# A mixture-of-experts kernel: slots from the third unit on, three picked last slots, and another order of scatters on GpSimd

## The chip, the core and the metric

The kernel runs on one core of one Trainium2 chip. The metric is the device time of one execution in microseconds (us). A run of three or five rounds alternates the kernel studied with the kernel before on the same chip. A ratio is the mean time of one kernel's runs over that of the other's in the same rounds, so it is not quite the ratio of the medians that are quoted beside it.

## The reference, cut to what matters

```python
# x: (8, 3584, 192) float32; a causal depthwise convolution of width 7, softmaxed weights per head
x = attn(x, weight).reshape(28672, 192)
e_idx  = argmax(x @ w_gate, axis=1)                    # 8 experts, one per row
gate_w = softmax(x @ w_gate)[row, e_idx]
eom    = sigmoid(x @ w_output_gate)
for e in range(8):
    mask = e_idx == e
    out[mask] = gate_w * eom[:, e] * (relu(x[mask] @ w1[e]) @ w2[e])     # 192 -> 1024 -> 192
```

## The kernel before

The rows are worked on in 16 units of 1792 rows. For each unit a *front* computes the convolution and the gates (front_a), then ranks the rows by expert and scatters them as pairs of rows, eight scatters a unit, to a stream in DRAM that is sorted by expert (front_b). A *slot* loads 512 rows of one expert from that stream with a transposing DMA (xa, xb), runs the two layers on TensorE and scatters 4 times 128 rows to the output. A unit's iteration has four slots, each in four quarters, with the fronts of later units between the quarters:

```python
for u in range(1, NU):                      # NU = 16; unit 0 and 1 are prepared before
    todo = []
    for e, bap, inv in plans.pop(u):        # four slots; eight after the last unit
        base = reg(bap, [ET.SP], E * CAP - TT)
        todo.append((e, inv, slot_load(base, u)))
    fa = front_a(u + 2) ...
    fb = front_b(u + 1) ...
    for k, (e, inv, xab) in enumerate(todo):
        s = Slot(xab, w_at(e * WE), inv)
        for q in range(4):
            s.first(q)                      # first layer, a quarter
            drain(fa, 1)
            if prev is not None:
                prev.second(q)              # second layer of the slot before; output scatters
            drain(fb, 1)                    # may make the data of one input scatter
        prev = s
```

All scatters are issued by GpSimd, in program order. Before, a made input scatter was put into a queue and issued one at a time ahead of an output scatter:

```python
                for j in (q - 1, q):        # in second(q), q odd
                    emit_in()               # at most one waiting input scatter
                    i = nc.gpsimd.indirect_dma_start(out=out, ..., in_=self.y[:, j, :])
```

A slot's load waits until all scatters of its unit have landed. Rows left after the static slots go through a loop whose count is known only at run time: it picks the expert with most rows left, computes one slot with nothing beside it, and repeats.

## Time and profile before

| | before |
|---|---|
| median of 3 runs (lowest to highest) | 780.03 us (779.94 to 781.78) |
| profiled run, span | 772.0 us |
| TensorE busy, mean granted clock | 655.4 us (85%), 0.947 |
| first slot matmul | 86.1 us |
| last matmul of the static slots | 742.1 us |
| last output scatter issued | 764.88 us |

The main stage lies between the first slot matmul and the last matmul of the static slots. Ahead of it is the start-up, after it the loop's one pass.

### The profile page before, as it was taken

The page shows a single profiled execution, that of the slowest core. Times are in us where ns is not written, and L with a number is a line of the kernel's source. Part 1 is how long each engine was busy: PE and PEld are TensorE (multiplying, and loading weights), DVE is VectorE, ACT ScalarE, POOL GpSimd, SP SyncE. Part 2 cuts the span into 40 slices and gives each one's busy share as a digit, 9 for nine tenths or more (in the row PEclk, how much of TensorE's full clock was granted, in tenths as well). Part 3 has the DMA queues.
Part 4 walks back from the last instruction along what each step waited for, and adds up shares of the span by engine and source line. Part 5 has one row for each costly group of instructions (what it writes and reads, how often), then busy time and mean ns, then how long its engine had stood idle before and what let it go on. Part 6 is the DMA issues. An engine that isn't in the chain of part 4 may idle for free. (4 is left out here: it accounts for less than half of the span.)

```text
span 772.0 us, 14134 instructions
## 1 busy us (share of the span) xinstructions
PE 655.4 (85%) x4948; PEld 436.2 (57%) x4948; DVE 406.5 (53%) x1298; ACT 366.5 (47%) x581; POOL 411.5 (53%) x425
## 2 busy tenths in 40 slices
PE   3866498989989898989989898989989898869953
PEld 1524165665757475656747475656757575547632
DVE  7425183836566383837556383837566474802220
ACT  0657153554535363545536364545546354436621
POOL 1436145473747465473737465563737375656652
PEclk9978599999999999999999999999999999989987
DMA  7999933253535343252535343442532313234110
GB/s 152 231 238 203 142 101 108 72 160 75 144 102 143 103 133 104 69 155 73 152 92 139 99 127 106 101 133 62 157 88 74 93 61 110 70 102 114 48 41 9
DMA packets 132359, 86.59 MB, mean 112 GB/s; under 512 B 88427, under 2 KB 122455, under 8 KB 132288
## 3 DMA queue, kind: packets, MB, share of 16 engines
q1 hardware_dynamic: 102656, 42.35, 23.4%
q0 software_dynamic: 28736, 43.31, 20.5%
q8 instruction: 39, 0.64, 0.4%
q14 instruction: 32, 0.26, 0.1%
q10 hardware_dynamic: 896, 0.03, 0.1%
HBM read 35.80 MB, written 44.43 MB: 104 GB/s over the span
## 5 line engine op out<-in xcount | busy, mean ns | idle before, releaser
L579 POOL DMA_INDIRECT out_dram<-y,oi x260 | 262.7, 1011 | 242.1 <-issue 179.0
L547 ACT ACTIVATE ht<-pp 128x1024 f16<-128x1024 f32 x195 | 199.3, 1022 | 183.9 <-PE pp L541 183.9
L539 PE MATMUL pp<-xa,wres 128*128 128x512 f16 x520 | 203.0, 390 | 61.1 <-DMA xa<-xcg_sorted 61.1
L558 PE MATMUL pyt<-wres,ht 128*128 128x192 f16 (+1 forms) x2080 | 220.9, 250 | 2.9 <-DVE ht L545 2.9
L558 PEld LDWEIGHTS <-ht 128*128 128x128 f16 x2080 | 182.7, 99 | 67.1 <-issue 37.0
L541 PE MATMUL pp<-xb,wres 128*128 128x512 f16 x520 | 202.2, 389 | 12.2 <-DMA xb<-xcg_sorted 12.2
L457 POOL DMA_INDIRECT xcg_sorted<-xs,du x128 | 130.1, 1017 | 89.4 <-ACT xs L278 42.2
L290 PE MATMUL pf<-xt,band 118*112 118x384 f32 x256 | 115.3, 543 | 19.5 <-DMA xt<-in_x_dram 14.1
L539 PEld LDWEIGHTS <-wres 128*128 128x128 f16 (+1 forms) x520 | 51.4, 99 | 112.4 <-DMA xa<-xcg_sorted 41.2
L545 DVE TENSOR_SCALAR ht<-pp 128x1024 f16<-128x1024 f32 x65 | 79.2, 1219 | 59.2 <-PE pp L541 59.2
L569 ACT COPY y<-pyt 128x384 f32<-128x384 f32 x130 | 62.4, 480 | 93.9 <-PE pyt L558 84.1
L280 DVE COPY cv<-pf 112x384 f32<-112x384 f32 x54 | 29.2, 541 | 89.3 <-PE pf L290 89.3
L290 PEld LDWEIGHTS pf<-xt,band 118*112 118x112 f32 x256 | 48.0, 195 | 48.9 <-DVE band L133 13.6
L541 PEld LDWEIGHTS <-wres 128*128 128x128 f16 (+1 forms) x520 | 51.8, 100 | 37.6 <-issue 8.2
L572 DVE TENSOR_SCALAR oi<-pyt 128x4 uint32<-128x4 f32 x65 | 10.5, 162 | 115.8 <-ACT y L569 110.3
L439 PE MATMUL pf<-xrow,pm 112*128 112x194 f16 x512 | 64.6, 247 | 6.9 <-DVE pm L423 4.5
L418 DVE TENSOR_TENSOR xrow<-cv,gs 112x384 f16<-112x384 f32 x128 | 64.7, 545 | 0.0
L423 DVE TENSOR_SCALAR pm<-pos,pos 112x256 f16<-112x256 f16 x256 | 64.6, 324 | 0.0
L304 PEld LDWEIGHTS pf<-identf,cv 112*128 112x128 f32 x384 | 43.6, 141 | 17.4 <-DVE cv L280 2.2
L278 ACT COPY cv<-pf 112x384 f32<-112x384 f32 x74 | 33.9, 479 | 40.1 <-PE pf L290 25.0
L304 PE MATMUL pf<-identf,cv 112*128 112x112 f32 x384 | 51.5, 260 | 0.5 <-ACT cv L278 0.4
L278 ACT CAST xs<-pf 128x388 f16<-128x388 f32 x76 | 37.2, 489 | 28.8 <-PE pf L439 20.2
(132 smaller groups left out, 425.0 us busy)
## 6 DMA issues: line engine op xcount, KB each, us to landing
xt<-in_x_dram SPq DMA_DIRECT2D x8, 1344.0 KB
xt<-in_x_dram SPq DMA_DIRECT2D x8, 1260.0 KB
out_dram<-y,oi POOLq DMA_INDIRECT x260, 2.7
wres<-in_moe_w_dram POOLq DMA_DIRECT2D x8, 384.0 KB, 10.5
wres<-in_moe_w_dram POOLq DMA_DIRECT2D x8, 256.0 KB, 11.5
xcg_sorted<-zrow SPq DMA_DIRECT2D x8, 256.0 KB
xcg_sorted<-xs,du POOLq DMA_INDIRECT x128, 3.2
xa<-xcg_sorted SPq DMA_TRANSPOSE x65
```

What stands on the lines that cost most here:

```text
L278: nc.scalar.copy(out=o, in_=i)
L290: nc.tensor.matmul(pc[0:BT, 0:NB * GH], band[0:KI, h, :], xt[0:KI, :, h * GH:(h + 1) * GH], start=True, stop=True)
L304: nc.tensor.matmul(pt[:, j * BT:(j + 1) * BT], cvf[0:BT, m * 2 * D + i * 128:m * 2 * D + (i + 1) * 128], identf[0:BT, 0:BT], is_transpose= ...
L418: nc.vector.tensor_tensor(out=xr[P, k:k + 2, 0:D], in0=cv[P, k:k + 2, :], in1=gs[P, k:k + 2].unsqueeze(2).to_broadcast([BT, 2, D]), op=ALU ...
L423: nc.vector.tensor_scalar(out=pms[i][P, l, :], in0=pos16[P], scalar1=pos[P, l * NG + i:l * NG + i + 1], scalar2=None, op0=ALU.is_equal)
L457: i = nc.gpsimd.indirect_dma_start(out=xcg2, out_offset=bass.IndirectOffsetOnAxis(ap=du[:, i:i + 1], axis=0), in_=xs.rearrange("p r w -> p ...
L539: nc.tensor.matmul(pp[:, j, :], self.w(fc * 128, 128), self.xa, start=True, stop=False)
L541: nc.tensor.matmul(pp[:, j, :], self.w(F + fc * 128, 128), self.xb, start=False, stop=True)
L545: nc.vector.tensor_relu(out=ht, in_=pp)
L547: nc.scalar.activation(out=ht, in_=pp, func=AF.Relu)
L558: nc.tensor.matmul(self.pp[:, o:o + D], self.ht[fc // 2][:, fc % 2, q * 128:(q + 1) * 128], self.w(2 * F + fc * D, D), start=(fc == 0 and ...
L579: i = nc.gpsimd.indirect_dma_start(out=out, out_offset=bass.IndirectOffsetOnAxis(ap=self.oi[:, j:j + 1], axis=0), in_=self.y[:, j, :], in_ ...
```

## The change

The slots begin with the third unit (U0 = 2), so that they are fuller; the three last slots are picked among the experts with most rows left, in the overlapped part of the program; GpSimd gets its scatters in the order in which their data is made. There are twelve buffers (xs) for input scatters in place of six, and the experts' weights are issued two at a time in place of four and then two.

```diff
-    NXS = 6
+    NXS = 12
...
+    def emit_out():
+        while pout:
+            y, oi, j = pout.popleft()
+            i = nc.gpsimd.indirect_dma_start(out=out, ..., in_=y[:, j, :], ...)
...
+    U0 = 2
     def plan(u):
-        if u == 0:
+        if u < U0:
             return []
-        p = plan_half((u + 1) % 2, "a")
+        p = plan_half(u % 2, "a")
...
-    for u in range(2):                     # fronts ahead of all slots
+    for u in range(U0 + 1):
...
-        if u == 0:
-            for e in range(EH, EH + 2):
-                load_w(e)
+        if u < U0:
+            load_w(2 + 2 * u)
+            load_w(3 + 2 * u)
...
-    for u in range(1, NU):
+    for u in range(U0, NU):
...
+        if u == NU - 1:
+            for sel, bap, inv in [pick() for _ in range(ND)]:          # ND = 3
+                base = reg(bap[0:1, 0:1], [ET.SP], E * CAP - TT)
+                todo.append((sel, inv, slot_load(base, u)))
...
                 if prev is not None:
                     prev.second(q)
+                    emit_out()
                 drain(fb, 1)
+                emit_in(len(pend))
```

pick() is the arithmetic that stood in the loop's body, on VectorE; the loop stays for what is left.

More of the change, by code (lines that the diff above doesn't have):

```diff
@@ L60 @@
     WE = F + F + FCH * D
+    ND = 3
     BIG = float(1 << 30)
@@ L201, with load_w @@
     nc.vector.tensor_copy(out=pos16, in_=poi.rearrange("p r j -> p (r j)"))
+    wres = const.tile([128, E * WE], FP16)
+    def load_w(e):
+        o = e * WE
+        nc.gpsimd.dma_start(wres[:, o:o + F], moe_w1[e, 0:128, :])
+        nc.gpsimd.dma_start(wres[0:64, o + F:o + 2 * F], moe_w1[e, 128:D, :])
+        nc.gpsimd.dma_start(
+            wres[:, o + 2 * F:o + WE].rearrange("p (c d) -> p c d", d=D),
+            moe_w2[e].rearrange("(c p) d -> p c d", p=128))
+    load_w(0)
     GE = NG * E
@@ L244 @@
     nc.vector.memset(zrow, 0.0)
-    wres = const.tile([128, E * WE], FP16)
-    def load_w(e):
-        o = e * WE
-        nc.gpsimd.dma_start(wres[:, o:o + F], moe_w1[e, 0:128, :])
-        nc.gpsimd.dma_start(wres[0:64, o + F:o + 2 * F], moe_w1[e, 128:D, :])
-        nc.gpsimd.dma_start(
-            wres[:, o + 2 * F:o + WE].rearrange("p (c d) -> p c d", d=D),
-            moe_w2[e].rearrange("(c p) d -> p c d", p=128))
     def zero_w(e):
@@ L469, in emit_in @@
             n -= 1
+    pout = deque()
+    def emit_out():
+        while pout:
+            y, oi, j = pout.popleft()
+            i = nc.gpsimd.indirect_dma_start(
+                out=out, out_offset=bass.IndirectOffsetOnAxis(ap=oi[:, j:j + 1], axis=0),
+                in_=y[:, j, :], in_offset=None, bounds_check=N - 1, oob_is_err=False)
+            nodep(i, "out", ("out",))
+            last[0] = "out"
     def nodep(i, group, others):
@@ L502, in plan_half, with pick @@
         return [(e0 + i, bu[0:1, i:i + 1], iu[:, i, :]) for i in range(EH)]
+    U0 = 2
     def plan(u):
-        if u == 0:
+        if u < U0:
             return []
-        p = plan_half((u + 1) % 2, "a")
+        p = plan_half(u % 2, "a")
         if u == NU - 1:
-            p += plan_half(u % 2, "b")
+            p += plan_half((u + 1) % 2, "b")
         return p
+    def pick():
+        lv = pr.tile([128, E], FP32, tag="lv", name="lv")
+        nc.vector.tensor_tensor(out=lv, in0=R, in1=DN, op=ALU.subtract)
+        lm = pr.tile([128, 1], FP32, tag="lm", name="lm")
+        nc.vector.tensor_reduce(out=lm, in_=lv, axis=AX.X, op=ALU.max)
+        oh = pr.tile([128, E], FP32, tag="oh", name="oh")
+        nc.vector.scalar_tensor_tensor(out=oh, in0=lv, scalar=lm, in1=rev,
+                                       op0=ALU.is_equal, op1=ALU.mult)
+        om = pr.tile([128, 1], FP32, tag="om", name="om")
+        nc.vector.tensor_reduce(out=om, in_=oh, axis=AX.X, op=ALU.max)
+        sel = pr.tile([128, 1], U32, tag="sel", name="sel", bufs=ND)
+        nc.vector.tensor_scalar(out=sel, in0=om, scalar1=-float(WE), scalar2=float(E * WE),
+                                op0=ALU.mult, op1=ALU.add)
+        nc.vector.tensor_scalar(out=oh, in0=oh, scalar1=om, scalar2=None, op0=ALU.is_equal)
+        bt = pr.tile([128, E], FP32, tag="bt", name="bt")
+        nc.vector.scalar_tensor_tensor(out=bt, in0=R, scalar=-float(TP), in1=DN,
+                                       op0=ALU.add, op1=ALU.min)
+        nc.vector.scalar_tensor_tensor(out=bt, in0=bt, scalar=2.0, in1=oh,
+                                       op0=ALU.mult, op1=ALU.mult)
+        bo = pr.tile([128, 1], FP32, tag="bo", name="bo")
+        nc.vector.tensor_reduce(out=bo, in_=bt, axis=AX.X, op=ALU.add)
+        bou = pr.tile([128, 1], U32, tag="bou", name="bou", bufs=ND)
+        nc.vector.tensor_copy(out=bou, in_=bo)
+        tk1 = pr.tile([128, 1], FP32, tag="tk1", name="tk1")
+        nc.vector.tensor_scalar(out=tk1, in0=lm, scalar1=float(TP), scalar2=None, op0=ALU.min)
+        nc.vector.scalar_tensor_tensor(out=DN, in0=oh, scalar=tk1, in1=DN,
+                                       op0=ALU.mult, op1=ALU.add)
+        nc.vector.tensor_scalar(out=tk1, in0=tk1, scalar1=-2.0, scalar2=float(TT),
+                                op0=ALU.mult, op1=ALU.add)
+        iv1 = pr.tile([128, 4], FP32, tag="iv1", name="iv1")
+        nc.vector.tensor_scalar(out=iv1, in0=rowf, scalar1=tk1, scalar2=BIG,
+                                op0=ALU.is_lt, op1=ALU.mult)
+        iu1 = pr.tile([128, 4], U32, tag="iu1", name="iu1", bufs=ND)
+        nc.vector.tensor_copy(out=iu1, in_=iv1)
+        return sel, bou, iu1
@@ L576, in second @@
                                             op=ALU.bitwise_or)
-                for j in (q - 1, q):
-                    emit_in()
-                    i = nc.gpsimd.indirect_dma_start(
-                        out=out, out_offset=bass.IndirectOffsetOnAxis(
-                            ap=self.oi[:, j:j + 1], axis=0),
-                        in_=self.y[:, j, :], in_offset=None,
-                        bounds_check=N - 1, oob_is_err=False)
-                    nodep(i, "out", ("out",))
-                    last[0] = "out"
+                pout.extend((self.y, self.oi, j) for j in (q - 1, q))
     def reg(ap, engines, hi):
@@ L609, in chain @@
             yield from g
-    for e in range(EH):
-        load_w(e)
+    load_w(1)
     drain(front_a(0))
     ze = 0
-    for u in range(2):
+    for u in range(U0 + 1):
         fa, fb = front_a(u + 1), front_b(u)
@@ L626 @@
         emit_in(len(pend))
-        if u == 0:
-            for e in range(EH, EH + 2):
-                load_w(e)
+        if u < U0:
+            load_w(2 + 2 * u)
+            load_w(3 + 2 * u)
     while ze < E:
@@ L639 @@
             base = reg(bap, [ET.SP], E * CAP - TT)
-            todo.append((e, inv, slot_load(base, u)))
+            todo.append((w_at(e * WE), inv, slot_load(base, u)))
+        if u == NU - 1:
+            for sel, bap, inv in [pick() for _ in range(ND)]:
+                base = reg(bap[0:1, 0:1], [ET.SP], E * CAP - TT)
+                todo.append((sel, inv, slot_load(base, u)))
         fa = front_a(u + 2) if u + 2 < NU else iter(())
         fb = front_b(u + 1) if u + 1 < NU else iter(())
-        for k, (e, inv, xab) in enumerate(todo):
-            if u == 1 and k < 2:
-                load_w(EH + 2 + k)
-            s = Slot(xab, w_at(e * WE), inv)
+        for k, (w, inv, xab) in enumerate(todo):
+            if u == U0 and k < 2:
+                load_w(E - 2 + k)
+            if not callable(w):
+                w = w_dyn(reg(w[0:1, 0:1], [ET.PE], (E - 1) * WE))
+            s = Slot(xab, w, inv)
             for q in range(4):
@@ L658 @@
         prev.second(q)
+        emit_out()
     lf = const.tile([128, E], FP32)
@@ L676 @@
     with tc.For_i(0, rn, 1):
-        lv = pr.tile([128, E], FP32, tag="lv", name="lv")
-        nc.vector.tensor_tensor(out=lv, in0=R, in1=DN, op=ALU.subtract)
-        lm = pr.tile([128, 1], FP32, tag="lm", name="lm")
-        nc.vector.tensor_reduce(out=lm, in_=lv, axis=AX.X, op=ALU.max)
-        oh = pr.tile([128, E], FP32, tag="oh", name="oh")
-        nc.vector.scalar_tensor_tensor(out=oh, in0=lv, scalar=lm, in1=rev,
-                                       op0=ALU.is_equal, op1=ALU.mult)
-        om = pr.tile([128, 1], FP32, tag="om", name="om")
-        nc.vector.tensor_reduce(out=om, in_=oh, axis=AX.X, op=ALU.max)
-        sel = pr.tile([128, 1], U32, tag="sel", name="sel")
-        nc.vector.tensor_scalar(out=sel, in0=om, scalar1=-float(WE), scalar2=float(E * WE),
-                                op0=ALU.mult, op1=ALU.add)
-        nc.vector.tensor_scalar(out=oh, in0=oh, scalar1=om, scalar2=None, op0=ALU.is_equal)
-        bt = pr.tile([128, E], FP32, tag="bt", name="bt")
-        nc.vector.scalar_tensor_tensor(out=bt, in0=R, scalar=-float(TP), in1=DN,
-                                       op0=ALU.add, op1=ALU.min)
-        nc.vector.scalar_tensor_tensor(out=bt, in0=bt, scalar=2.0, in1=oh,
-                                       op0=ALU.mult, op1=ALU.mult)
-        bo = pr.tile([128, 1], FP32, tag="bo", name="bo")
-        nc.vector.tensor_reduce(out=bo, in_=bt, axis=AX.X, op=ALU.add)
-        bou = pr.tile([128, 1], U32, tag="bou", name="bou")
-        nc.vector.tensor_copy(out=bou, in_=bo)
-        tk1 = pr.tile([128, 1], FP32, tag="tk1", name="tk1")
-        nc.vector.tensor_scalar(out=tk1, in0=lm, scalar1=float(TP), scalar2=None, op0=ALU.min)
-        nc.vector.scalar_tensor_tensor(out=DN, in0=oh, scalar=tk1, in1=DN,
-                                       op0=ALU.mult, op1=ALU.add)
-        nc.vector.tensor_scalar(out=tk1, in0=tk1, scalar1=-2.0, scalar2=float(TT),
-                                op0=ALU.mult, op1=ALU.add)
-        iv1 = pr.tile([128, 4], FP32, tag="iv1", name="iv1")
-        nc.vector.tensor_scalar(out=iv1, in0=rowf, scalar1=tk1, scalar2=BIG,
-                                op0=ALU.is_lt, op1=ALU.mult)
-        iu1 = pr.tile([128, 4], U32, tag="iu1", name="iu1")
-        nc.vector.tensor_copy(out=iu1, in_=iv1)
+        sel, bou, iu1 = pick()
         base = reg(bou[0:1, 0:1], [ET.SP], E * CAP - TT)
@@ L716 @@
             s.second(q)
+            emit_out()
 _INS = ['x', 'weight', 'moe_w_gate', 'moe_w_output_gate', 'moe_w1', 'moe_w2']
```

## The prediction

> **What bounds the kernel now.** I read the page's header and slices first, then the waits of TensorE, of the other engines and of the DMA queue, then the timeline at three places: the start, one boundary between two units, and the end.
>
> The page:
>
> ```profile
> span 772.0 us, 14134 instructions
> PE 655.4 (85%) x4948; PEld 436.2 (57%) x4948; DVE 406.5 (53%) x1298; ACT 366.5 (47%) x581; POOL 411.5 (53%) x425
> ...
> PE   3866498989989898989989898989989898869953
> ...
> PEclk9978599999999999999999999999999999989987
> DMA  7999933253535343252535343442532313234110
> ```
>
> TensorE sets the pace in the middle, where its slices show 8 and 9. Slices 1 to 5 are a start-up with DMA at 9, and the last two are a tail with everything low. So there are three stages, and each needs its own account.
>
> The waits of the whole run (the last line is from the DMA queue's own list):
>
> ```profile
> POOL out_dram L579 <- issue: 179.0, 164, 13.2
> PE pp L539 <- DMA xa<-xcg_sorted: 61.1, 16, 13.4
> ACT xs L278 <- DMA xcg_sorted<-xs,du: 8.6, 2, 7.4
> ...
> SPq L516 <- DMA xcg_sorted<-xs,du: 253.0, 32, 20.2
> ```
>
> In the main stage TensorE has one big wait: the transposed load of a slot's rows (xa). There are 16 such waits: 13.4 us at the first slot, 7.0 us in the loop at the end, and 14 at the boundaries between units (40.8 us together by the same list cut to 110 to 740 us). The load itself waits for the scatters (xs to xcg_sorted) to land.
>
> One boundary, from the timeline:
>
> ```profile
> 161.92 0.56 DVE L280 CAST xs<-pf 128x388 f16<-128x388 f32 x1 [0.16 <-PE pf L439]
> ...
> 167.96 0.98 POOL L457 DMA_INDIRECT xcg_sorted<-xs,du  x1 [0.30 <-issue]
> ...
> 170.22 0.82 PE L558 MATMUL pyt<-wres,ht 128*128 128x192 f16 x8
> 170.48 1.15 SPq L516 DMA_TRANSPOSE xa<-xcg_sorted  x1
> ...
> 173.67 0.39 PE L539 MATMUL pp<-xa,wres 128*128 128x512 f16 x1 [2.63 <-DMA xa<-xcg_sorted]
> ```
>
> The unit's last scatter data is ready at 162.5. GpSimd issues that scatter only at 167.96: it is 5.5 us behind. The load starts 2.5 us later, and TensorE 3.2 us after that. I read the same five times at the 14 boundaries from 129.9 to 687.2: the lag is 5.3 to 6.1 us, the stall 2.3 to 3.0 us, except 6.4 us at the last one, where the unit has less TensorE work.
>
> The end:
>
> ```profile
> 740.59 1.48 PE L558 MATMUL pyt<-wres,ht 128*128 128x192 f16 x16
> ...
> 746.85 0.98 POOL L579 DMA_INDIRECT out_dram<-y,oi  x1 [0.30 <-issue]
> ...
> 749.07 0.59 PE L539 MATMUL pp<-xa,wres 128*128 128x512 f16 x1 [7.00 <-DMA xa<-xcg_sorted]
> ...
> 759.14 2.14 PE L558 MATMUL pyt<-wres,ht 128*128 x16
> 761.01 1.00 POOL L579 DMA_INDIRECT out_dram<-y,oi  x1 [13.18 <-issue]
> ...
> 764.88 0.98 POOL L579 DMA_INDIRECT out_dram<-y,oi  x1 [0.30 <-issue]
> ```
>
> The static slots end on TensorE at 742.1 and on GpSimd at 746.85. Then the loop runs once, with nothing to overlap it. Its last output scatter is issued at 764.88, and 7.1 us later the span ends.
>
> **What the Trainium skill says.** "Perfetto Trace Analysis", section "DMA Instruction — SWDGE (GPSIMD)": the window shown for such a DMA ends when its descriptors are written, not when data has moved. The trace agrees: 0.98 us shown, 2.4 us at least to landing. "DMA: Bandwidth & Descriptors", section "Two DMAs through the same engine are not ordered": a reader of written data must wait for the writer's completion semaphore. So issue-to-load time (2.5 us here) stays whatever the order. "TensorE: Matmul & The Clock Gate", section "What's actually happening": the array drops to half clock after an idle window of some 3.4 us and needs as long to recover. The trace partly agrees: after this 2.63 us stall eight output matmuls show 1.49 us in place of 0.82, and slot matmuls beyond 0.5 us follow 9 of the 14 boundaries, not all.
>
> **The change part by part.**
>
> *Slots.* I counted the routing of the reference's own inputs: pairs of rows per unit, block group and expert, rounded up, taken off 256 a slot. For the kernel before this gives 64 static slots and one loop pass of 108 pairs: 65, and the page's 260 output scatters are 65 times 4. For the changed kernel: slots begin with unit 2, so 14 units of 4, 4 more after the last, and 3 picked. At the picks 104, 102 and 82 pairs are left with three experts and none with the others. So 63 slots, and the loop runs zero times.
>
> *Main stage.* Before, from the first slot matmul at 86.1 to 742.1 there are 656.0 us: unit 1's iteration 43.8, twelve full ones 517.7 (43.1 each), unit 14's 39.6, unit 15's 54.9 with eight slots. After, unit 1's iteration is gone and three slots are added to the last. A slot costs TensorE 4 times (0.87 + 0.66) = 6.1 us, from start-to-start times in the timeline (161.72 to 162.59 for a quarter's first matmuls, 162.97 to 163.63 for its second). The picked slots address weights by a register. In the loop pass that did so, 16 output matmuls took 2.14 us against 1.48 just before, and ten 1.47, so I add 1.6 us for each: 18.4 + 4.8 = 23.2 us.
>
> *GpSimd's order.* Scatters are 1.286 us apart when GpSimd is busy (0.98 + 0.30). The order list shows the first-to-last-scatter stretch of a unit as X OO XX OO XX OO XX OO X in place of X OO X O X O X O X O X O X (X a scatter to xcg_sorted, O one of output). Both have 8 outputs between the first X and the last: 16 operations, at least 15 times 1.286 = 19.3 us, against 21.2 us observed (146.73 to 167.96) and 16 us between the first and last data. The order can only take away waits at the queue's head. I replayed the trace's own ready times through both orders for 13 boundaries: the last X moves up 0.3 to 1.0 us, mean 0.66. So the stall shrinks from some 2.6 to 1.9 us, and the 13 boundaries that the changed kernel has give 9 us. This is the claim that I am least at ease with.
>
> *Main sum.* 517.7 + 39.6 - 9 + 54.9 + 23.2 = 626.4 us, which is 29.6 less than 656.0. The picks are 3 times 14 VectorE operations of some 0.2 us, 8 us, at the start of unit 15, where VectorE lies idle in the 6.4 us stall: nothing.
>
> *The loop.* Without a pass the last output scatter is that of 746.85: 764.88 - 746.85 = 18.0 us less.
>
> *Start-up.* A third unit is prepared before any slot. A bare round costs 18 us (57.9 to 75.8 for the second). Against it stands the hole between the first two rounds, 46.9 to 57.9: ScalarE waited 7.43 us at 53.9 for one of six xs buffers whose scatter had not landed under full DMA, and the clock dropped to half. Twelve buffers and weights loaded two experts at a time instead of four should close most of it: I take 8 us. Weights stay six before the first slots and two beside them, so the first slot load should still take long (7.8 us before). DMA has one more unit of x (1.34 MB) and 8 scatters to move, some 9 us at its rate, and there were about 9 us of idle DMA time before 86. Net +10: first slot matmul at 96.
>
> *Sum.* -29.6 - 18.0 + 10 = -37.6 us; 780.0 - 37.6 = 742.4.
>
> **The rivals.** (1) The order removes the whole lag. Then the 13 stalls go, some 36 us, with their slow-clock time: 742 becomes about 710 to 715. For it: the lag of 5.3 us is twice the stall. Against: GpSimd has 19.3 us of work for 16 us of data. (2) DMA sets the start-up, so the third round adds its full 18 us, or more as the early expert's load gets in the way of the first x: 742 becomes 750 to 755. For it: DMA share around 1 from 20 to 55 us. Against: the stall at 53.9 is on buffers. (3) GpSimd becomes the bound: consecutive input scatters get a nop between them. 24 scatters at 1.286 are 31 us of a 43 us unit, so a small rise is swallowed, at most 5 us. (4) The fuller slots leave more than three experts at the end and the loop runs: plus 18. The count speaks against it.
>
> **The range.** The sure parts (two slots less, no loop pass) give about -47 before the start-up, which would have to cost 32 us to come to the 2% line (764.4). I predict **742 us**, 8 in 10 between **729 and 755**; faster by over 2%: **0.94**, within: **0.05**, slower: **0.01**. The low end leaves room for a stall that shrinks more than the replay says, the high end for a start-up at full cost.
>
> **What would show it.** 252 output scatters and 504 first-layer matmuls per operand, no loop pass. First slot matmul at 92 to 104. Lag of the last scatter 4.3 to 5.2 us and TensorE's waits for xa of 1.5 to 2.3 us at 13 boundaries. No wait of ScalarE for a scatter's buffer at the start. Picked slots of 7 to 8 us. I am wrong if the loop still runs, if the first slot starts after 110, or if the boundary stall is gone or larger.

## The result, and the profile after

The changed kernel takes 743.82 us (median of 4 runs, 741.66 to 748.41) against 779.99 us of the kernel before; the ratio is 0.9544 (95% interval 0.9488 to 0.9599). The page of its profiled run:

```profile
span 739.9 us, 13994 instructions
...
PE 637.5 (86%) x4844; PEld 425.1 (57%) x4844; DVE 401.2 (54%) x1308; ACT 363.9 (49%) x583; POOL 407.2 (55%) x417
...
PE   3888449899898989899898989989898997779994
...
DMA  9969993425453533525353352535423224254210
```

TensorE is busy in nearly the same share of a shorter span (86% and 85%). The tail is short now (one low slice in place of two), and the middle still alternates between 8 and 9. The page counts 252 output scatters and 504 first-layer matmuls per operand: 63 slots and no pass of the loop, as counted. In the list of waits (us in total, times, longest):

```profile
PE pp L593 <- DMA xa<-xcg_sorted: 51.0, 14, 17.0
```

There are 13 boundaries between units and the first slot, and the first slot is the longest wait, 17.0 us in place of 13.4. An ordinary boundary, from the timeline (start, us, engine, line, operation, and in brackets the idle time before it):

```profile
345.02 0.49 ACT L281 CAST xs<-pf 128x388 f16<-128x388 f32 x1
...
350.99 0.98 POOL L460 DMA_INDIRECT xcg_sorted<-xs,du  x1 [0.30 <-ACT ht L601]
...
353.53 1.14 SPq L570 DMA_TRANSPOSE xa<-xcg_sorted  x1
...
356.40 0.39 PE L593 MATMUL pp<-xa,wres 128*128 128x512 f16 x1 [2.31 <-DMA xa<-xcg_sorted]
```

The last scatter's data is ready at 345.5 and GpSimd issues it at 351.0, still 5.5 us behind; the load follows after 2.5 us and TensorE waits 2.31 us. Averaged over the ordinary boundaries (all but the last) the lag of the last scatter behind its data went from 5.4 to 5.2 us and the stall of TensorE from 2.64 to 2.28 us. So the boundary is almost what it was. The start:

```profile
87.07 0.98 POOL L460 DMA_INDIRECT xcg_sorted<-xs,du  x1 [0.30 <-issue]
...
91.11 2.70 SPq L570 DMA_TRANSPOSE xa<-xcg_sorted  x1
91.16 1.00 POOL L211 DMA_DIRECT2D wres<-in_moe_w_dram  x1
...
101.73 0.58 PE L593 MATMUL pp<-xa,wres 128*128 128x512 f16 x1 [17.02 <-DMA xa<-xcg_sorted]
```

The third unit's data was ready at 85.2 us (75.6 for the second unit before). From there to the first slot matmul it takes 16.5 us, where it took 10.5: the scatter is issued 1.8 us late, the load follows 4.0 us later, and the load itself takes 10.6 us, with weights on GpSimd's queue beside it. This way is not the same in every run: in the five profiled runs on ordinary chips that leave the start as it is in the changed kernel, the scatter is 1.8 to 4.6 us late, the load takes 7.9 to 12.0 us, and the first slot matmul comes at 99.0 to 103.6 us.

The time by stages of the two profiled runs, us:

| | before | predicted | after |
|---|---|---|---|
| first slot matmul | 86.1 | 96 | 101.7 |
| to the last matmul of the static slots | 656.0 | 626.4 | 627.9 |
| of that: twelve full units from the second slot unit on (before), all twelve (after) | 517.7 | 509.4 | 509.9 |
| of that: unit 15, with eight or eleven slots | 54.9 | 78.1 | 78.1 |
| from there to the end of the span | 29.9 | 11.9 | 10.3 |

### The profile page after: what moved, and what is told of

Its sections match the earlier page's. It is cut to its first block, busy times and chain, and to the rows that moved or that the text cites. A ratio compares the mean times of both kernels' runs of the same rounds, so it can differ in the third digit from the quotient of the medians.

```text
span 739.9 us, 13994 instructions
## 1 busy us (share of the span) xinstructions
PE 637.5 (86%) x4844; PEld 425.1 (57%) x4844; DVE 401.2 (54%) x1308; ACT 363.9 (49%) x583; POOL 407.2 (55%) x417
## 5 line engine op out<-in xcount | busy, mean ns | idle before, releaser
L480 POOL DMA_INDIRECT out_dram<-y,oi x252 | 258.7, 1027 | 213.5 <-issue 160.0
L601 ACT ACTIVATE ht<-pp 128x1024 f16<-128x1024 f32 x189 | 193.3, 1023 | 170.0 <-PE pp L595 170.0
L593 PE MATMUL pp<-xa,wres 128*128 128x512 f16 x504 | 195.0, 387 | 51.9 <-DMA xa<-xcg_sorted 51.0
L612 PE MATMUL pyt<-wres,ht 128*128 128x192 f16 (+1 forms) x2016 | 214.2, 248 | 1.9 <-DVE ht L599 1.9
L612 PEld LDWEIGHTS <-ht 128*128 128x128 f16 x2016 | 176.6, 99 | 64.4 <-issue 33.7
L595 PE MATMUL pp<-xb,wres 128*128 128x512 f16 x504 | 194.0, 385 | 9.1 <-DMA xb<-xcg_sorted 9.1
L293 PE MATMUL pf<-xt,band 118*112 118x384 f32 x256 | 111.4, 532 | 16.1 <-DMA xt<-in_x_dram 12.3
L593 PEld LDWEIGHTS <-wres 128*128 128x128 f16 (+1 forms) x504 | 49.3, 98 | 100.0 <-issue 35.7
L626 DVE TENSOR_SCALAR oi<-pyt 128x4 uint32<-128x4 f32 x63 | 10.2, 162 | 114.0 <-ACT y L623 103.6
L595 PEld LDWEIGHTS <-wres 128*128 128x128 f16 (+1 forms) x504 | 49.8, 99 | 33.1 <-issue 3.6
L283 DVE COPY cv<-pf 112x384 f32<-112x384 f32 x48 | 26.0, 542 | 78.7 <-PE pf L293 78.7
L442 PEld LDWEIGHTS <-pm 112*128 112x128 f16 x512 | 41.8, 97 | 18.5 <-DVE pm L426 14.8
```

The costliest lines, as they stand in the source:

```text
L293: nc.tensor.matmul(pc[0:BT, 0:NB * GH], band[0:KI, h, :], xt[0:KI, :, h * GH:(h + 1) * GH], start=True, stop=True)
L442: nc.tensor.matmul(ps[:, r * XW:(r + 1) * XW], pm[P, l, r * 128:(r + 1) * 128], xr[P, l * NG + i, :], start=(r == 0 and l == 0), stop=(r = ...
L480: i = nc.gpsimd.indirect_dma_start(out=out, out_offset=bass.IndirectOffsetOnAxis(ap=oi[:, j:j + 1], axis=0), in_=y[:, j, :], in_offset=Non ...
L593: nc.tensor.matmul(pp[:, j, :], self.w(fc * 128, 128), self.xa, start=True, stop=False)
L595: nc.tensor.matmul(pp[:, j, :], self.w(F + fc * 128, 128), self.xb, start=False, stop=True)
L601: nc.scalar.activation(out=ht, in_=pp, func=AF.Relu)
```

## The experiments

The theory after the result: the count of slots and the lost loop pass pay most, the order on GpSimd pays little because the stall at a boundary comes from the number of scatters that GpSimd has to issue there, which the new order keeps, and the start-up pays back part through the weights beside the first load. The rivals are that the order or the later start is the main part, or that the stall is the latency of the DMAs.

### A first call on an unlike chip

Four kernels of five rounds came first: the changed kernel again, and it with one of three edits each.

```diff
# the old order
 def emit_out():
     while pout:
+        emit_in()
         y, oi, j = pout.popleft()
...
                 drain(fb, 1)
-                emit_in(len(pend))
```

```diff
# six buffers
-    NXS = 12
+    NXS = 6
```

```diff
# the last two experts' weights late
-            if u == U0 and k < 2:
-                load_w(E - 2 + k)          # ahead of the first and second slot
             s = Slot(xab, w, inv)
             for q in range(4): ...
+            if u == U0 and k >= 2:
+                load_w(E - 4 + k)          # after the third and fourth slot
```

> The changed kernel unaltered, as the anchor for the three runs beside it. Expected: 742 to 745 us, ratio to the kernel before 0.954, first slot matmul near 101.7 us, TensorE's stall for xa 2.3 us on average at the 12 ordinary boundaries.

> The changed kernel with the old order on GpSimd (one input scatter ahead of each output scatter, X OO X O X O ...), all else kept. My theory: the order only takes away waits at the head of the queue, so the lag of the last input scatter goes back to 5.3 to 5.5 us, the stall at an ordinary boundary from 2.3 to 2.6 us, a full unit from 42.5 to 43.1 us: 5 to 9 us slower than the changed kernel, some 751 us. Rival A (the order is a main part of the gain): 15 us or more slower. Rival B (the order does nothing, GpSimd's throughput is the same): within 2 us.

> The changed kernel with 6 in place of 12 xs buffers. My theory: ScalarE waits again for a buffer whose scatter has not landed at the start of the second round, so the first slot matmul comes 4 to 8 us later (106 to 110 us) and the time is 4 to 8 us more. Rival: with the weights spread out, scatters land in time and six buffers are enough; then the first slot stays near 102 us and the time within 2 us, and the closing of the hole was due to the weights.

> The changed kernel with the weights of the last two experts issued after the third and fourth slot, in place of ahead of the first. My theory: the first slot's load shares DMA with those weights (10.6 us from issue to TensorE in place of 3.2); without them it takes 4 to 6 us, so the first slot matmul comes at 95 to 97 us and the time falls by 4 to 7 us to some 738 us. Rival: the queue is full of x, scatters and the other weights anyway, or the late weights hold up GpSimd's scatters in the first unit: no gain within 2 us.

On this chip the kernel before takes 801.55 us, in place of 780 on the others, and the changed kernel 781.17 (ratio 0.9754), with the old order 777.0 (0.9703), with six buffers 782.22 (0.9758), with late weights 786.53 (0.9835). A full unit of the changed kernel takes 44.8 us on average, against 42.5, at a similar granted clock (0.952 against 0.957 over the run), and the waits are scattered over all engines. The boundary stall is 0.25 us, with a lag of 3.6 us: from a unit's first scatter data to its last it takes 19 to 22 us there, in place of 16, so that GpSimd has time to catch up. The old order was not slower here, as expected, but 4 us faster, with intervals that overlap. What slows this chip was not found, so its times are not used to judge the order. Its start-ups can be compared with each other, up to the first slot matmul:

| on the unlike chip | first slot matmul, us |
|---|---|
| changed kernel | 102.2 |
| six buffers | 108.1 |
| late weights | 94.7 |

Six buffers cost 5.9 us there and late weights gain 7.5 us, both about as expected. With six buffers ScalarE waits again for scatters to land before it may write a buffer, 4.9 us of it at 92.4, so in the third round and not, as expected, in the second:

```profile
ACT xs L281 <- DMA xcg_sorted<-xs,du: 6.4, 3, 4.9
```

In the changed kernel on the same chip the view lists none. In the total times neither expectation holds: six buffers are 1 us slower where 4 to 8 were expected, and late weights are 5 us slower where they were to gain 4 to 7. For the late weights the trace names a place where the gain went: TensorE waits 5.85 us at the start of the next unit, put down to a weight DMA that GpSimd had issued only at 142. For the buffers it stays open.

### The old order, and four experts ahead, on an ordinary chip

The changed kernel and the old order were run again, with the weights of four experts issued ahead of the first round and of one more after each of the first two rounds:

```diff
-    load_w(0)                     # ahead of the first constants
...
-    load_w(1)
+    for e in range(4):
+        load_w(e)
     drain(front_a(0))
...
-            load_w(2 + 2 * u); load_w(3 + 2 * u)
+            load_w(4 + u)
```

> The changed kernel unaltered, as the anchor on the chip of this call; the first call fell on a chip on which the kernel before needs 801 us, with waits scattered over all engines and hardly a boundary stall, and so says nothing on the order. If this chip is like those of the other calls: ratio 0.954 to the kernel before, first slot matmul near 102 us, boundary stall 2.3 us.

> The changed kernel with the old order on GpSimd, on a chip that shows the boundary stall. My theory: lag back from 5.1 to 5.4 us, stall from 2.3 to 2.6 us, 4 to 9 us slower than the anchor. Rival A (the order is a main part of the gain): 15 us or more slower. Rival B (the order does nothing): within 2 us.

> The changed kernel with the weights of four experts issued ahead of the first round, as before, and one expert after each of the two next rounds; twelve xs buffers stay. My theory of the prediction: the early weights made scatters land late and so the hole; with twelve buffers the hole stays closed, and the first slot matmul moves by under 4 us from the anchor's 102 us. Rival (DMA sets the start-up, whatever the order of the loads): no difference, within 1 us. Second rival (spreading the weights was the part that paid): first slot at 107 us or later.

The anchor takes 744.67 us (ratio 0.9564, interval 0.9527 to 0.9601), as before. With the old order it is 754.21 us (0.9684, interval 0.965 to 0.9717): the order is worth 9.5 us, at the upper edge of what was expected. But the way it pays is not the expected one. The lag is 5.5 against 5.2 us and the stall 2.60 against 2.44 us, 0.16 us a boundary, most of it from a single stall of 4.01 us. The view of stretches for the eleven full units of units 3 to 13 shows where the rest is (us, then busy time of TensorE, its weight loads, VectorE, ScalarE and GpSimd with instructions; then clock, DMA share, GB/s). The anchor:

```profile
143.80:613.20 469.40, 434.38 (x3366) 294.44 (x3366) 277.30 (x862) 233.72 (x368) 270.53 (x265) 0.97 0.40 110
```

The old order:

```profile
143.70:622.90 479.20, 441.07 (x3366) 297.04 (x3366) 277.28 (x862) 234.04 (x368) 268.77 (x265) 0.96 0.39 108
```

The same 3366 matmuls are busy 6.7 us longer with the old order, and TensorE idles 3.1 us longer (38.1 against 35.0). So two thirds of these 9.8 us are a slower clock after the stalls, at 0.96 in place of 0.97: by the clock records in the two traces, 41 us of this stretch are at half clock with the old order and 24 us in the anchor. Slot matmuls of more than 0.5 us follow 11 of 13 boundaries with the old order and 7 of 13 in the anchor. In the six runs of each the mean clock is 0.943 to 0.952 with the old order, 0.948 to 0.959 in the anchor, and the anchor's slowest run, 750.23 us, is the one at 0.948. Why stalls that are so little longer are followed by half clock more often is not shown.

Four experts ahead give 742.95 us (0.9539, interval 0.9508 to 0.9571) with the first slot at 97.3 us, against 99.0 in the anchor. No worth of loading the weights two at a time is seen: the intervals overlap, and 1.7 us is within the 99.0 to 103.6 us over which the first slot matmul of an unaltered start scatters.

### The loop back, and the start with the second unit

```diff
# two picks
-    ND = 3
+    ND = 2
```

```diff
# second unit
-    U0 = 2
+    U0 = 1
-    ND = 3
+    ND = 1
-        p = plan_half(u % 2, "a")
+        p = plan_half((u + 1) % 2, "a")       # and the other half for "b"
-            load_w(2 + 2 * u)
-            load_w(3 + 2 * u)
+            for e in range(2, 6):
+                load_w(e)
```

> The changed kernel with two picked slots in place of three, so that the loop runs once for the last 82 pairs. My theory: one overlapped picked slot less is 6.1 + 1.6 = 7.7 us less, the loop pass is 18 us more: 9 to 12 us slower than the changed kernel, some 754 us. Rival: a pass of the loop costs little more than a picked slot, so within 4 us.

> Slots from the second unit on, as before, with one picked slot (by count 64 + 1 = 65 slots, no loop pass), the rest as in the changed kernel. My theory: starting with the third unit saves only two slots, because the unit that it prepares ahead is no longer overlapped. Here the first slot comes 18 to 20 us earlier (82 to 84 us), one more iteration adds 42.5 us, two picked slots less take 15.6 us off: 5 to 9 us slower than the changed kernel, some 750 us. Rival: starting with the third unit is the main gain of the change, so this one loses 15 us or more.

Both ran beside the kernel before at 780.88 us. With two picked slots the loop runs once for the last 82 pairs: 754.57 us, ratio 0.9676 against the 0.9544 of the changed kernel, 10 us more (of 780.88), as expected. Its output scatters show the pass:

```profile
739.80 0.98 POOL L480 DMA_INDIRECT out_dram<-y,oi  x1 [13.91 <-issue]
...
743.66 0.98 POOL L480 DMA_INDIRECT out_dram<-y,oi  x1 [0.30 <-issue]
```

GpSimd is idle for 13.91 us ahead of the pass's first output scatter. A pass costs more than two picked slots do.

Starting with the second unit gives 757.84 us, ratio 0.9706, that is 13 us more than the changed kernel, where 5 to 9 were expected and 15 or more would have meant the rival. So neither forecast held. The main stage behaves as expected: a full unit is 42.7 us. The start does not: the first slot comes at 90.5 us in place of 82 to 84, with its data ready at 68.5 and the last scatter issued 9.6 us later, behind the weights of four experts on GpSimd's queue. These four in a row are this run's own, since the changed kernel puts two between rounds, so they may account for the 6.5 to 8.5 us by which the first slot is late. An estimate from these numbers: with the weights spread, 4.5 to 6.5 of the 13 us would be left. What the later start is worth by itself is thus not shown; it is at most about a third of the gain. Nor is the third round hidden: in the profiled run of the changed kernel the second round's last data is ready at 69.3 us and the third's at 85.2, which is 15.9 us for a round.

### What makes the boundary stall

If GpSimd's throughput is the cause, fewer operations between the first input scatter of a unit and its last must cure it. The output scatters of each unit's third slot can wait: they block nothing.

```diff
                 if prev is not None:
                     prev.second(q)
-                    emit_out()
+                    if k != 2 or u == NU - 1:
+                        emit_out()
                 drain(fb, 1)
                 emit_in(len(pend))
+                if q == 3:
+                    emit_out()
```

The second kernel below has this and the late weights told above, and the third has the weights of the last four experts late, after the second to the fourth slot of the first slot unit.

> The changed kernel with the four output scatters of each unit's third slot held back until the unit's last input scatter is issued (X OO XX OO XXXXX then 12 O). My theory: GpSimd's backlog makes the boundary stall. With 4 in place of 8 outputs among the 8 inputs its queue needs 11 times 1.286 = 14 us for 16 us of data, so the lag of the last input scatter falls from 5 to under 1.5 us, its load can start 3 to 4 us earlier, and TensorE's 2.3 us stall is gone at the 12 ordinary boundaries, with the half-clock time after it: 25 to 38 us less, some 705 to 718 us. Rival A: the stall is set by the scatter's landing and the load's own latency (2.5 and 3.2 us) and shrinks only in part: 10 us less or under. Rival B: the 12 outputs that then come in one run fill the y buffers and hold TensorE up elsewhere: no gain.

> Both the held outputs and the late weights. If the two losses are separate (boundary stall, first load) their gains add: some 30 to 43 us less than the changed kernel, 700 to 714 us. If the late weights disturb GpSimd in the first unit, it is no better than the held outputs alone.

> Held outputs, and the weights of the last four experts (needed by the second slot unit only) issued during the first slot unit, in place of the last two. If the start-up is bound by DMA, first slot matmul at 90 to 94 us in place of 95.6, and the time 2 to 5 us below the run with held outputs and two late: ratio to the kernel before 0.867 to 0.871. If the weights now hold up GpSimd's input scatters in the first unit, its lag grows to over 2 us there, and the gain is lost.

Held outputs (on a chip where the kernel before takes 780.88 us, against 779.57 on the anchor's) give 689.08 us (ratio 0.8833, interval 0.8795 to 0.8871), 55 us less than the changed kernel (0.9544 less 0.8833, of 780.88), which is more than the 25 to 38 that were expected. One boundary of this run:

```profile
289.66 0.56 DVE L283 CAST xs<-pf 128x388 f16<-128x388 f32 x1 [0.16 <-PE pf L442]
290.50 0.98 POOL L460 DMA_INDIRECT xcg_sorted<-xs,du  x1 [0.42 <-DVE xs L283]
...
293.06 1.14 SPq L570 DMA_TRANSPOSE xa<-xcg_sorted  x1
```

The data is ready at 290.2 and the scatter is issued at 290.5. The load is on its way at 293.1, and TensorE does not wait for it: the next unit starts at 298.6 without a stall. The wait for xa is gone at all 12 ordinary boundaries and 0.98 us at the last one, where it was 6.61. The same eleven units in the view of stretches:

```profile
145.10:567.20 422.10, 420.02 (x3369) 289.92 (x3368) 275.85 (x858) 233.55 (x368) 270.15 (x265) 1.00 0.47 123
```

TensorE idles 2.1 us in place of the anchor's 35.0, and is busy 14.4 us less for the same matmuls, at a clock of 1.00, with no half clock in the trace from 110 to 680 us. So of the 47.3 us that these units gain, 32.9 are waits and 14.4 the half clock after them. The expectation had counted on 12 stalls of 2.3 us, 27.6 us, and on at most 10 us more. GpSimd's own work is the same (270.2 against 270.5 us busy): only 4 output scatters in place of 8 lie between a unit's first input scatter and its last. This settles the cause: the way from the last scatter to its load is 2.5 us at most boundaries, as before, and had that latency alone made the stall, it would still be there.

Held outputs and late weights together give 681.86 us (0.8733, interval 0.8695 to 0.8772), on the same chip 7.2 us less than the held outputs alone, and the first slot comes at 95.6 in place of 103.6. The gains add, as expected; the time is again lower than forecast (700 to 714). This is the fastest kernel, 13% below the kernel before and 8.5% below the changed one.

Four experts late give 683.89 us, ratio 0.8773 (interval 0.8739 to 0.8807), on another chip. The first slot comes at 91.2, as expected, but the time is no better. The boundary after the first slot unit shows why:

```profile
119.50 0.99 POOL L211 DMA_DIRECT2D wres<-in_moe_w_dram  x1
...
121.79 0.56 DVE L283 CAST xs<-pf 128x388 f16<-128x388 f32 x1 [0.16 <-PE pf L442]
...
124.73 0.98 POOL L460 DMA_INDIRECT xcg_sorted<-xs,du  x1 [0.30 <-issue]
...
129.73 1.14 SPq L570 DMA_TRANSPOSE xa<-xcg_sorted  x1
...
132.91 0.38 PE L593 MATMUL pp<-xa,wres 128*128 128x512 f16 x1 [2.01 <-DMA xa<-xcg_sorted]
```

A weight load now sits among the input scatters of the first slot unit. The last scatter is 2.4 us behind its data and needs 5.0 us to the load in place of 2.5, and the stall is back there. The first two units take 41.7 and 43.2 us, where the kernel with two late has 40.3 and 38.0. That is 6.6 us lost, against 4.4 us gained at the start: the second branch of what was expected.

## Why the prediction was right

Predicted were 742 us (729 to 755) and a gain of over 2%; measured are 743.82 us. Step by step:

- *Slots.* Right: 63, and no pass of the loop, by the counts of the page.
- *Main sum.* Right within 1.5 us of 626.4 (627.9). The parts agree too: the full units within 0.5 us, unit 15 with its register-addressed slots exactly.
- *The loop.* Right: the end comes 10.3 us after the last static matmul where 11.9 were implied, and the experiment that brings one pass back is 10 us slower, the 18 us of the pass less the picked slot.
- *GpSimd's order.* The amount was right (9 us predicted, 9.5 measured by undoing it), the mechanism only in part, so that the agreement is partly luck. (The old order is printed one O X short in the prediction; the trace has X OO X O X O X O X O X O X O X, with the 8 outputs that its sum uses.) The stall was said to shrink by 0.7 us a boundary; it shrank by 0.2 to 0.4, and where the order was undone two thirds of the loss were half clock after more of the boundaries. The prediction had listed the slow clock, but put no number on it for this step. That the order could not remove the lag, because GpSimd has 19.3 us of work for 16 us of data, was right.
- *Start-up.* Mis-sized: +10 was predicted, +15.6 measured in the profiled run, +12.9 in the anchor's. The data of the last round before the slots comes 9.7 us later, near the 10 of the sum, but from two terms that were each about 2 us off: the round takes 15.9 us and not 18, and the second round's data comes 6.3 us earlier and not 8. What the sum left out is the way from there to the first matmul, 16.5 in place of 10.5 us. The line "Weights stay six before the first slots and two beside them, so the first slot load should still take long (7.8 us before)" took it as unchanged, while it grew to 10.6 us, with a later issue and landing ahead of it. In the anchor the load is 7.9 us, as taken, and the last scatter is 4.5 us late instead, 3.0 of them a wait of GpSimd that the trace puts down to a weight DMA. Moving the two weights beside the first slots away leaves 2.6 to 2.7 us of the load and brings the first slot 7.5 to 8 us forward.
- *The hole.* It was credited to buffers and weights together. The wait of ScalarE for a buffer is gone, as the prediction said (8.6 us before, 0.6 after). The runs speak for the buffers: six bring the wait back and put the first slot 5.9 us later (one profiled run, on the unlike chip), while four experts ahead with twelve buffers have 0.3 us of it, and their first slot is no later than the anchor's.
- *Why the total came out.* That it is right within 2 us is luck. In spans the error is that of the start-up: 734.4 implied (772.0 less 37.6), 739.9 measured. Of the fall in the median, 36.2 us, the spans of the two profiled runs show 32.1, since the profiled run of before (773.92 us) was 6 us faster than its median. The two errors partly cancel in 742 against 743.8. The range would have held without this.
- *The rivals.* The second (a third round at its full 18 us or more) came about in part, with +12.9 to +15.6 at the first slot; the fourth (the loop runs) did not. The third (GpSimd as the bound through nops) did not come about; its busy time fell a little. The first was right on its premise and wrong on its means: the lag can be removed, not by the order, but by holding outputs back, and then it is worth 55 us, not the 30 or so that the prediction gave it. It had counted the 13 stalls and too little of what comes with them.

## What to carry to other kernels

When an engine waits at every round for data that passes through another engine's queue, count the operations of that queue between the first and the last piece of the data, and compare their sum with the time in which the data is made: if the sum is larger, an order that keeps them all there cannot take the lag away, and work that nobody waits for should be moved out of that stretch. A short stall of TensorE costs more than its length when the clock drops after it, so look at the busy time of the same matmuls, not only at the waits. A load that is moved away from a crowded start must not land in another queue's critical stretch, and a part of a change should be undone by itself, with all else kept, before it is credited.

## What the Trainium skill lacked or had wrong

- "TensorE: Matmul & The Clock Gate", section "What's actually happening", gives one idle window of some 3.4 us as what drops the clock. Here shorter stalls did it at times: in the changed kernel slow slot matmuls follow stalls of 1.8 to 2.6 us at 6 of 12 ordinary boundaries, and do not follow one of 3.05 us. (One matmul after each stall comes a wait for xb, of 1.3 us at most, so the idle times add up to more than the stall.) Without the stalls the eleven full units are busy 14.4 us less. No page gives a length at which shorter waits that recur drop the clock.
- "DMA: Bandwidth & Descriptors", section "Anatomy of one DMA — SWDGE (gpsimd) path", calls the time of descriptor generation "small, variable". Here an indirect scatter of 128 rows shows 0.98 us, for rows of 512 elements (2 bytes each) and of 192 (4 bytes) alike. No page gives the interval of scatters that queue, on which the boundary stall rests in this kernel: 1.286 us from one to the next.
- No page was found that tells of a chip that differs from others: one chip needed 801.55 us where two others needed 779.57 and 780.88 for the same kernel, with a unit of the changed kernel at 44.8 in place of 42.5 us.
